# A local attention with a gated convolution on one core: one order table for all engines, transposes in 64-row pieces, two banks for products

## The chip, the cores and the metric

One core of one Trainium2 chip. The metric is device time in microseconds (us) of one execution; the profile's span runs from the first to the last instruction. Engines: PE (TensorE: matrix products, transposes), DVE (VectorE), ACT (ScalarE), POOL (GpSimd), SP (SyncE, which here issues all DMAs). Each engine has its own list of instructions, in the order in which the kernel writes them; semaphores hold an instruction until its operands are there.

## The reference

Inputs q, k, v have 4 batches, 8 heads, 768 positions, 64 channels. Each query attends to the keys less than 16 positions away and to 24 summaries, one per block of 32 positions (the maximum of the block's keys, the mean of its values). The result goes through a gated convolution.

```
k_sum = max over blocks of k;  v_sum = mean over blocks of v
scores = q k^T / 8 where |i-j| < 16;   scores_s = q k_sum^T / 8 + log(32)
a = softmax over both (sum + 1e-9);    x = a @ [v ; v_sum], heads side by side: (4, 768, 512)
gate_pre[s] = sum over t=0..4 of conv_w[t] * x[s-4+t]   (zeros ahead of position 0)
out = (sigmoid(gate_pre) * (x @ w_val)) @ w_out
```

## The kernel before

**Tiles.** A group g is a third of a batch (256 positions; 12 groups), a unit u is one half of a group's heads (4 of 8; 24 units, u = 2g or 2g+1). A query tile has 64 positions and sees 120 columns of keys: its window and the 24 summaries, laid between the keys in two halves of 12. A row of 128 partitions holds two neighbouring query tiles (e = 0 in partitions 0 to 63, e = 1 in 64 to 127); a unit has 8 such rows of scores.

**Steps of a unit**, with the letters used from here on. S: 32 products of q and k, 64 rows by 64 columns by 120, on quarters of the array, into the two banks of `s`. N: score scaling, mask and row minimum, 8 custom instructions on DVE. E: 8 exponentials with row sums on ACT. R: reciprocal on DVE. M: two multiplications by it on POOL. T: 8 transposes of 128 by 120, in two lots of four, each into the one bank of `pt`; C: a copy of each lot to SBUF on ACT. X: 32 products with v, 64 columns each. H, F: two copies of x on ACT (rounded, full); L: the rest that rounding lost, on POOL. I: the convolution's first tap on ACT, A: four more taps for each of two head pairs, 8 instructions on DVE, in the one accumulator `g`; G: tanh on ACT.

**Steps of a group.** V: x @ w_val in two halves, 24 matmuls each (three products of rounded parts); gf: gate times V on DVE; gh, gl: its rounded part on ACT, the rest on POOL; O: the product with w_out, two halves of 12 matmuls; oe: its eviction on ACT, then the store. Group 0 computes V and O in full fp32. Further: block maxima of k (`ks` on DVE, `kc` on POOL), block sums of v (a tree `tr` on POOL, transposed on PE by VS), and the conversion of the weights, which arrive as 64-bit words (ACT, DVE, POOL).

**PSUM's eight banks:** `s` two, `pt` one, `x` one, `g` one, `pp` three in turn (V, O and the sums' transposes).

**Order.** Up to unit 7 it is written out by hand (L605 to L782), from there `step(s)` (L556) runs a fixed pattern: X of unit s-2 and O or V, S of unit s, the first half of T of unit s-1, V or O, the second half of T. So PE alternates T's halves with V and O, which have the array's full shape as well. V, O and their evictions come from a queue (`proj`, L511). `early_loads` and `late_loads` set the order of the DMAs on SP.

Of the kernel before, what the change touches and what calls it, by code (L numbers as in the profile page):

```python
# [45 lines left out]
LOADS = "k0 q0 m k1 q1 n0 i k2 q2 n1 k3 q3 n2 n3 v0 c Q w0 w1 w2 w3 v1"  # L46
UPB = NTH * NHP
LOAD_K = {1: (2, 2, 4, 5)}
LOAD_VT = {1: (2, 2, 5, 6)}
PREP_K = {1: (-1,) * 4}  # L50
PREP_V = {1: (-1,) * 4}
DVE_V = ((1, 3),)
for _b in range(2, B):
    LOAD_K[_b] = tuple(_b * UPB + w for w in (-5, -4, -3, -2))
    LOAD_VT[_b] = LOAD_K[_b]
    PREP_K[_b] = tuple(_b * UPB + w for w in (-3, -2, -1, 0))
    PREP_V[_b] = tuple(_b * UPB + w for w in (-4, -3, -2, -1))


@with_exitstack  # L60
def tile_attention_then_gated_conv(
# [23 lines left out]
    ps_p = ctx.enter_context(tc.tile_pool(name="ps_p", bufs=3, space=bass.MemoryType.PSUM))  # L85
# [11 lines left out]
    ktile = {}  # L97
    vtile = {}
    vTt = {}

    def load_q0(pr):
        nc.sync.dma_start(qbd[0][:, pr], qT[0, 0, :, pr])

    def load_q(g):
        b, th = divmod(g, NTH)
        nc.sync.dma_start(qbd[g % NQB], qT[b, th])

    def load_k(b, pr):
        t = ld.tile([P, KALLOC], F32, tag=f"k{pr}", name=f"k_{b}_{pr}")
        nc.sync.dma_start(t[:, :KTOT], kT[b, pr])  # L110
        ktile[b, pr] = t

    def load_vT(b, pr):
        t = ld.tile([P, S], F32, tag="vT", name=f"vT_{b}_{pr}")
        nc.sync.dma_start(t, vT[b, pr])
        vTt[b, pr] = t

    def load_v(g):
        b, th = divmod(g, NTH)
        t = ld.tile([VROWS, TPU, DM], F32, tag="v", name=f"v_{g}")  # L120
        for e in range(VP):
            nc.sync.dma_start(t[:, 2 * e : 2 * e + 2], vw[b, th, e])
        vtile[g] = t

    def prep_k(b, pr):
        t = ktile[b, pr]
        ks = wk.tile([P, NB], F32, tag="ks", name=f"ks_{b}_{pr}")
# [6 lines left out]
        )  # L134
        for half, n in ((0, NT // 2 + 1), (1, NT // 2)):
# [5 lines left out]
    vsT = {}  # L141
    vsum = {}

    def prep_v(b, pr):
# [10 lines left out]
        vsT[b, pr] = t  # L155

    def load_vT0(i):
        t = ld.tile([P, S], F32, tag=f"k{i}", name=f"vT_0_{i}")
        nc.sync.dma_start(t, vT[0, i])
        vTt[0, i] = t  # L160

    vpad = cpool.tile([P, NPR, 2, P], F32, tag="vpad", name="vpad")
    nc.gpsimd.memset(vpad, 0.0)
    vblk = {}

    def prep_v0(i):
        half = [
            [vpad[:, i, e, off : off + HB] for off in ((OFF_A, OFF_B) if e == 0 else (OFF_B, OFF_A))]
            for e in range(2)
        ]  # L170
        src = vTt.pop((0, i)).rearrange("p (h n c) -> p h n c", h=2, c=BLK)
        for h in range(2):
            nc.vector.tensor_reduce(half[0][h], src[:, h], AX.X, ALU.add)
            nc.gpsimd.tensor_copy(half[1][h], half[0][h])

    def place_vs0():
        for e in range(2):
            ps = ps_p.tile([P, DM], F32, tag="pp", name=f"vb_{e}")
            for pr in range(NPR):
                nc.tensor.transpose(ps[:, pr * P : pr * P + P], vpad[:, pr, e], ident)  # L180
            t = cpool.tile([KW, DM], F32, tag=f"vb{e}", name=f"vb{e}")
            nc.scalar.activation(t, ps[:KW], AF.Copy, scale=1.0 / BLK)
            vblk[e] = t

    def prep_vs(b):
        ps = ps_p.tile([P, DM], F32, tag="pp", name=f"vsp_{b}")
        for pr in range(NPR):
            nc.tensor.transpose(ps[:NB, pr * P : pr * P + P], vsT.pop((b, pr)), ident)
        t = wk.tile([NB, DM], F32, tag="vs", name=f"vs_{b}", bufs=1)
        nc.scalar.activation(t, ps[:NB, :], AF.Copy, scale=1.0 / BLK)  # L190
        vsum[b] = t

    def fill_vs(g):
        b = g // NTH
        vr = vtile[g].rearrange("p (t e) c -> p e t c", e=2)
        for e in range(2):
            for half in range(2):
                off = OFF_A if (e == half) else OFF_B
                src = vsum[b][half * HB : half * HB + HB] if b else vblk[e][off : off + HB]
                nc.sync.dma_start(  # L200
                    vr[off : off + HB, e],
                    src.unsqueeze(1).broadcast_to([HB, TPU // 2, DM]),
                )
# [48 lines left out]
    def conv_cw():
        if wide:
            to_f32(cwt.rearrange("p a k -> p (a k)"), wraw.pop("cw"), NPR * NK, "cw", 1)

    acts = dict(
        k=lambda i: load_k(0, i),
        q=load_q0,
        n=load_vT0,
        w=lambda i: load_w("wv", wv, i, wk, ("gh", "gl")[i % 2]),  # L260
        o=lambda i: load_w("wo", wo, i, (cpool, cpool, wk, wk)[i], ("raw", "vpad", "xh", "xl")[i]),
        v=load_v,
        m=lambda i: nc.sync.dma_start(mask, maskc),
        i=lambda i: nc.sync.dma_start(ident, identc),
        c=lambda i: load_cw(),
        Q=lambda i: load_q(1),
    )
    for a in LOADS.split():
        acts[a[0]](int(a[1]) if len(a) > 1 else 0)

    units = [(b, th, hp) for b in range(B) for th in range(NTH) for hp in range(NHP)]
    NG = B * NTH
    st = {}
    grp = {}

    def group(g):
        if g not in grp:
            grp[g] = dict(
                xh=wk.tile([P, NPR, SG], F32R, tag="xh", name=f"xh_{g}") if g else None,
                xl=wk.tile([P, NPR, SG], F32R, tag="xl", name=f"xl_{g}") if g else None,  # L280
                gt=wk.tile([P, NPR, SG], F32, tag="gt", name=f"gt_{g}"),
                xf=wk.tile([P, NPR, HALO + SG], F32, tag="xf", name=f"xf_{g}"),
            )
            halo = grp[g]["xf"][:, :, :HALO]
            if g % NTH == 0:
                nc.gpsimd.memset(halo, 0.0)
            else:
                nc.gpsimd.tensor_scalar(
                    halo, grp[g - 1]["xf"][:, :, SG:], 1.0, 1.0, ALU.mult, ALU.mult
                )  # L290
        return grp[g]

    def mm_s(u, r):
        b, th, hp = units[u]
        g = b * NTH + th
        if r == 0:
            st[u] = dict(
# [563 lines left out]
```

## Time and profile before

| | us |
|---|---|
| runs (3): median, lowest, highest | 265.61, 263.45, 267.11 |
| profiled execution: span | 262.0 |
| PE, DVE, ACT, POOL busy in it | 231.1, 185.1, 193.0, 151.8 |

For the profiled execution the profile gives its span, from the first to the last instruction; the runs' times are of whole executions, and their median is 3.6 us above that span. A busy share is the union of an engine's instructions. The page lists a matmul with its modelled end, so what a matmul costs in a row of them is read from the chain of waits, which gives the time from one piece to the next.

### The profile page before, as it was taken

Reading aid. Unit: us, or ns where it says so; the run is one execution under the profiler, and the core shown is the slowest. Engines: PE = TensorE matmul, PEld = TensorE weight load, DVE = VectorE, ACT = ScalarE, POOL = GpSimd, SP = SyncE. Lnnn points to the kernel's source line nnn. Section 1 sums busy time; section 2 is a strip of 40 time slices with the busy share of each in tenths; the row PEclk is TensorE's granted clock in tenths of the full one; section 3 lists DMA queues with packets and bytes.
Section 4 is the critical chain, followed back from the end, with each engine's and each line's share of the span. In section 5 each row is a group of like instructions: output and inputs, shape, how many; then the busy total and the mean of one; then the engine's idle time right before and its main releaser. Section 6 shows DMA issues by size and latency. Waiting matters only on the chain.

```text
span 262.0 us, 7326 instructions
## 1 busy us (share of the span) xinstructions
PE 231.1 (88%) x2652; PEld 193.6 (74%) x2652; DVE 185.1 (71%) x692; ACT 193.0 (74%) x619; POOL 151.8 (58%) x212
## 2 busy tenths in 40 slices
PE   1258977889596999999999999999999999997994
PEld 1146866756482689888988898889889988986883
DVE  1866999597966687779776967797778667843610
ACT  1448994966648889888987898889878988875211
POOL 2243087767465788878663888887544744461410
PEclk9999999999777799999999999999999999999999
DMA  6999998175501967726118998171184511111012
GB/s 192 402 404 410 354 354 305 17 290 188 170 8 26 319 238 241 267 51 247 44 22 257 363 329 290 22 280 44 17 261 108 192 58 27 40 43 40 14 70 80
DMA packets 17028, 46.39 MB, mean 177 GB/s; under 512 B 2368, under 2 KB 3392, under 8 KB 16992
## 3 DMA queue, kind: packets, MB, share of 16 engines
q1 hardware_dynamic: 16992, 45.93, 50.9%
q8 instruction: 21, 0.34, 0.5%
q14 instruction: 15, 0.12, 0.2%
HBM read 37.46 MB, written 6.29 MB: 167 GB/s over the span
## 4 chain that ended last, share of the span: by engine, by line
PE 75%; ACT 10%; POOL 5%; issue 4%; DVE 2%; DMA 2%; SPq 0%; POOLq 0%; ACTq 0%; DVEq 0%
PE out L491 27%; PE val L453 22%; PE s L311 9%; PE x L387 8%; PE pt L367 8%; ACT p L342 4%; DMA k<-in_kT_dram 2%; POOL xl L405 2%; POOL p L354 1%; ACT pts L371 1%; DVE sn L328 1%; ACT wv L241 1%; ACT xf L403 1%; DVE ks L129 1%; POOL k L139 1%
## 5 line engine op out<-in xcount | busy, mean ns | idle before, releaser
L428 DVE SCALAR_TENSOR_TENSOR g<-xf,cwt,g 128x256 f32<-128x256 f32 x192 | 93.9, 489 | 13.9 <-ACT g L419 8.0
L342 ACT ACTIVATE p<-sn,nm 128x120 f32<-128x120 f32 x192 | 73.2, 386 | 10.9 <-DVE nm L328 10.9
L354 POOL TENSOR_TENSOR p<-p,ri 128x480 f32<-128x480 f32 x48 | 47.0, 1001 | 42.1 <-DVE ri L351 41.7
L328 DVE CUSTOM_DVE_ANT_0 sn<-s,mask 128x120 f32<-128x120 f32 x192 | 40.9, 278 | 33.3 <-PE s L311 33.3
L453 PE MATMUL val<-xh,wv 128*128 128x256 f32 x352 | 51.8, 289 | 0.7 <-ACT xh L402 0.7
L491 PE MATMUL out<-wo,gh 128*128 128x512 f32 x176 | 49.2, 418 | 2.0 <-ACT wo L241 1.2
L453 PEld LDWEIGHTS val<-xh,wv 128*128 128x128 f32 x352 | 45.6, 192 | 1.6 <-ACT xh L402 1.1
L405 POOL TENSOR_TENSOR xl<-xf,xh 128x512 fp32r<-128x512 f32 x22 | 28.3, 1288 | 23.3 <-ACT xf L403 23.3
L367 PE MATMUL pt<-ident,p 128*120 128x128 f32 x192 | 31.5, 289 | 11.0 <-ACT pts L371 7.6
L491 PEld LDWEIGHTS out<-wo,gh 128*128 128x128 f32 x176 | 32.1, 193 | 11.0 <-POOL wo L242 3.4
L311 PE MATMUL s<-k,qbd 64*64 64x120 f32 x768 | 27.7, 282 | 10.9 <-POOL k L139 10.9
L342 ACT ACTIVATION_READ_ACCUMULATOR p<-sn,nm 128x1 f32 x192 | 36.7, 191 | 0.0
L371 ACT COPY pts<-pt 120x512 f32<-120x512 f32 x48 | 27.6, 575 | 10.3 <-PE pt L367 10.3
L367 PEld LDWEIGHTS pt<-ident,p 128*120 128x120 f32 x192 | 21.7, 142 | 16.6 <-issue 7.3
L387 PEld LDWEIGHTS x<-pts,v 120*64 120x64 f32 x768 | 27.0, 141 | 9.2 <-issue 8.1
L476 POOL TENSOR_TENSOR gl<-gf,gh 128x512 fp32r<-128x512 f32 x22 | 28.5, 1298 | 6.6 <-ACT gh L467 6.6
L311 PEld LDWEIGHTS s<-k,qbd 64*64 64x64 f32 x768 | 20.9, 139 | 14.4 <-POOL k L139 12.6
L453 PE MATMUL val<-xl,wv 128*128 128x256 f32 x176 | 29.6, 288 | 1.8 <-POOL xl L405 1.7
L387 PE MATMUL x<-pts,v 120*64 120x64 f32 x768 | 30.7, 229 | 0.6 <-ACT g L419 0.5
L436 ACT ACTIVATE gt<-g 128x512 f32<-128x512 f32 x24 | 14.4, 599 | 22.0 <-DVE g L428 22.0
L153 POOL TENSOR_TENSOR vT<-vT 128x384 f32<-128x384 f32 (+3 forms) x44 | 25.6, 581 | 2.6
L453 PEld LDWEIGHTS val<-xl,wv 128*128 128x128 f32 x176 | 24.8, 191 | 2.6 <-POOL xl L405 2.1
(53 smaller groups left out, 268.2 us busy)
## 6 DMA issues: line engine op xcount, KB each, us to landing
v<-in_vw_dram SPq DMA_DIRECT2D x24, 512.0 KB
k<-in_kT_dram SPq DMA_DIRECT2D x16, 478.0 KB
vT<-in_vT_dram SPq DMA_DIRECT2D x16, 384.0 KB
out_dram<-ob SPq DMA_DIRECT2D x23, 256.0 KB
qbd<-in_qT_dram SPq DMA_DIRECT2D x11, 512.0 KB
raw_wv<-in_wv_dram SPq DMA_DIRECT2D x4, 512.0 KB
raw_wo<-in_wo_dram SPq DMA_DIRECT2D x4, 512.0 KB
v<-vs SPq DMA_DIRECT2D x36, 48.0 KB
```

The costliest lines, as they stand in the source:

```text
L311: nc.tensor.matmul(st[u]["sp"][64 * e : 64 * e + 64, h, c * KW : c * KW + KW], qbd[g % NQB][64 * h : 64 * h + 64, pr, i * QT : i * QT + QT ...
L328: nc.vector.tensor_tensor_reduce(s["sn"][:, n, :], s["sp"][:, h, c * KW : c * KW + KW], mask[:, mv, :], -1.0 / math.sqrt(D), 3.0e38, ALU.a ...
L342: nc.scalar.activation(s["p"][:, n, :], s["sn"][:, n, :], AF.Exp, bias=s["nm"][:, n : n + 1], scale=-1.0, accum_out=s["rs"][:, n : n + 1],)
L354: nc.gpsimd.tensor_tensor(s["p"][:, w], s["p"][:, w], ri[:, w].unsqueeze(2).broadcast_to([P, TPU, KW]), ALU.mult,)
L367: nc.tensor.transpose(s["pt"][:KW, i, :], s["p"][:, TPU * r + i, :], ident)
L371: nc.scalar.copy(s["pts"][:, TPU * r : TPU * r + TPU], s["pt"][:KW])
L387: nc.tensor.matmul(dst, v[:KW, i, c0 : c0 + D], src, start=True, stop=g > 0)
L405: nc.gpsimd.tensor_tensor(G["xl"][:, prs, :], x[:, prs, HALO:], G["xh"][:, prs, :].bitcast(F32), ALU.subtract)
L428: nc.vector.scalar_tensor_tensor(gt[:, r], x[:, pr, o : o + SG], cwt[:, pr, o : o + 1], gt[:, r], ALU.mult, ALU.add,)
L453: nc.tensor.matmul(pp[:, r], w, x, start=(n == 0), stop=(n == len(terms) - 1))
L476: nc.gpsimd.tensor_tensor(G["gl"][:, cos, :], gf, G["gh"][:, cos, :].bitcast(F32), ALU.subtract)
L491: nc.tensor.matmul(pp, x, w, start=(n == 0), stop=(n == len(terms) - 1))
```

## The change

All helper functions are cut into small operations, one per engine and piece, and named by a token. A table `ORDER` of 1148 tokens gives their order, for all engines and for the DMAs; a loop at the end of the kernel emits them. `step`, `proj`, the loads' functions and the order written out by hand are gone. Counts of operations stay, with these exceptions and moves:

- T: each row of a unit is transposed as two pieces of 64 rows by 120 columns, 16 per unit, all in one go. Pieces of e = 0 go to one bank, those of e = 1 to a second; `pt` has two banks in one buffer.
- C: one copy per e (half the queries of all 8 rows) instead of one per lot of four rows. X takes the tiles of e = 0 first.
- `pp` has two banks instead of three.
- N and E come in pairs, taps one by one, and the DMAs of one v tile apart, in the table's order.

```diff
-    ps_p = ctx.enter_context(tc.tile_pool(name="ps_p", bufs=3, space=bass.MemoryType.PSUM))
+    ps_p = ctx.enter_context(tc.tile_pool(name="ps_p", bufs=2, space=bass.MemoryType.PSUM))
...
-        s["pt"] = ps_t.tile([P, TPU, P], F32, tag="pt", name=f"pt_{u}_{r}")
-        for i in range(TPU):
-            nc.tensor.transpose(s["pt"][:KW, i, :], s["p"][:, TPU * r + i, :], ident)
...
-        nc.scalar.copy(s["pts"][:, TPU * r : TPU * r + TPU], s["pt"][:KW])
...
+    def op_T(u):
+        pt = once(("pt", u), lambda: ps_t.tile([P, 2, NP, QT], F32, tag="pt", name=f"pt_{u}"))
+        for n in range(NP):
+            for e in range(2):
+                w = slice(QT * e, QT * e + QT)
+                nc.tensor.transpose(pt[:KW, e, n, :], tiles["p", u][w, n, :], ident[w, w])
+
+    def op_C(u, e):
+        pts = wt(("pts", u), [KW, NP, P], "pts")
+        nc.scalar.copy(pts[:, :, QT * e : QT * e + QT], tiles["pt", u][:KW, e])
+
+    def op_X(u):
...
+        for i in (0, 2, 1, 3):
+            for r in range(2):
                 for h in range(2):
...
+    for token in ORDER.split():
+        name, *at = token.split(".")
+        ops[name](*(int(a) for a in at))
```

A token is a step's letter and its numbers: unit (or group) and piece; `k`, `q`, `n`, `v`, `w`, `o` are loads of k, q, transposed v, v, w_val, w_out, `m` the mask, `i` the identity, `f` the fill of v with block sums, `h` the convolution's halo. The table's beginning, and PE's part of it from T(9) to X(16) (a digit after the dot is the piece):

```
k.0.0 mset k.0.1 q0.0 k.0.2 q0.1 m k.0.3 q0.2 ks.0.0 n.0.1 kc.0.0 ks.0.1 q0.3 S.0.0 q.1 kc.0.1 c
ks.0.2 S.0.1 n.0.2 N.0.1 n.0.3 kc.0.2 E.0.1 N.0.0 N.0.3 w.0 N.0.2 E.0.2 i ks.0.3 S.1.0 E.0.3 n.0.0
...
PE: T.9 S.12 V.3.1 V.3.0 S.13 X.8 T.10 O.2.1 X.9 S.14 O.2.0 VS.2 T.11 S.15 X.10 V.4.1 V.4.0 T.12
X.11 S.16 T.13 O.3.1 O.3.0 S.17 T.14 X.12 V.5.1 V.5.0 S.18 X.13 O.4.1 O.4.0 S.19 T.15 X.14 V.6.0
V.6.1 X.15 T.16 S.20 O.5.0 O.5.1 VS.3 X.16
```

After X(23) PE has O.9.0 V.10.0 V.11.0 V.11.1 O.10.1 O.10.0 O.11.0 O.11.1; before, it had O, V, O, V, O, O, O there.

## Rows read from the trace of the kernel before

**Rows 1.** Page, part 1: busy time, share of the span and instructions of each engine.

```profile
PE 231.1 (88%) x2652; PEld 193.6 (74%) x2652; DVE 185.1 (71%) x692; ACT 193.0 (74%) x619; POOL 151.8 (58%) x212
```

**Rows 2.** Busy time by stretch: until X(6), until X(23), the rest; header names the columns.

```profile
core 0: us, PE busy (x) PEld busy (x) DVE busy (x) ACT busy (x) POOL busy (x), PEclk, DMA share, GB/s
0.00:89.00 89.00, 63.26 (x716) 47.01 (x718) 65.81 (x232) 60.26 (x196) 46.64 (x76) 0.92 0.68 243
89.00:235.20 146.20, 146.20 (x1804) 128.68 (x1804) 110.96 (x445) 124.69 (x410) 100.06 (x132) 1.00 0.48 161
235.20:262.00 26.80, 21.62 (x140) 17.93 (x139) 8.36 (x17) 8.04 (x15) 5.11 (x4) 1.00 0.14 50
```

**Rows 3.** Chain of waits in order of time, one steady unit: start, us, what.

```profile
106.46 1.08 PE x L387 x32
107.54 0.98 PE s L311 x32
108.52 0.58 PE pt L367 x4
109.11 2.85 PE val L453 x24
111.95 0.44 PE pt L367 x4
112.39 2.81 PE out L491 x12
115.20 1.08 PE x L387 x32
```

**Rows 4.** The same chain: X(6), X(23), the last products, the last eviction.

```profile
88.92 1.08 PE x L387 x32
...
235.81 0.69 PE x L387 x16
...
250.04 8.41 PE out L491 x36
258.52 0.39 ACT ob L500
```

**Rows 5.** Groups by line and shape, DVE: busy us, mean ns of one.

```profile
L428 DVE SCALAR_TENSOR_TENSOR g<-xf,cwt,g 128x256 f32<-128x256 f32 x192 | 93.9, 489 | 13.9 <-ACT g L419 8.0
...
L328 DVE CUSTOM_DVE_ANT_0 sn<-s,mask 128x120 f32<-128x120 f32 x192 | 40.9, 278 | 33.3 <-PE s L311 33.3
...
L129 DVE TENSOR_REDUCE ks<-k 128x24 f32<-128x768 f32 x16 | 14.9, 942 | 4.1 <-DMA k<-in_kT_dram 4.0
...
L460 DVE SCALAR_TENSOR_TENSOR gf<-gt,val 128x512 f32<-128x512 f32 x24 | 15.9, 665 | 8.9 <-ACT gt L436 3.9 <-PE val L453 3.5 <-PE out L491 1.6
```

**Rows 6.** Timeline of the start: start us, us, engine, line, operation.

```profile
3.98 0.95 DVE L129 TENSOR_REDUCE ks<-k 128x24 f32<-128x768 f32 x1 [3.98 <-DMA k<-in_kT_dram]
...
6.64 0.28 DVE L328 CUSTOM_DVE_ANT_0 sn<-s,mask 128x120 f32<-128x120 f32 x1 [1.70 <-PE s L311]
...
22.79 0.34 PE L387 MATMUL x<-pts,v 120*64 120x64 f32 x4
```

**Rows 7.** Busy time by stretch, 10 to 20 us; columns as in group 2.

```profile
10.00:20.00 10.00, 4.92 (x51) 3.46 (x43) 7.01 (x35) 4.87 (x22) 3.61 (x11) 1.00 1.03 402
```

**Rows 8.** The chain of waits: eight exponentials and their sums on ACT.

```profile
63.88 3.13 ACT p L342 x16
```

**Rows 9.** Groups by line and shape, PE weight loads of X and T.

```profile
L387 PEld LDWEIGHTS x<-pts,v 120*64 120x64 f32 x768 | 27.0, 141 | 9.2 <-issue 8.1 <-ACT g L419 0.8 <-ACT pts L371 0.4
...
L367 PEld LDWEIGHTS pt<-ident,p 128*120 128x120 f32 x192 | 21.7, 142 | 16.6 <-issue 7.3 <-POOL p L354 6.0 <-POOL vT L153 1.0
```

**Rows 10.** Timeline of PE after a wait of 3.17 us: four transposes.

```profile
69.07 1.08 PE L367 MATMUL pt<-ident,p 128*120 128x128 f32 x4 [3.17 <-ACT pts L371]
```

**Rows 11.** Busy time by stretch, 70 to 80 us.

```profile
70.00:80.00 10.00, 8.99 (x100) 7.84 (x100) 7.07 (x13) 4.31 (x9) 5.01 (x9) 0.75 0.19 70
```

More of the change, by code (lines that the diff above doesn't have):

```diff
@@ L45 @@
 FP32_G = (0,)
-LOADS = "k0 q0 m k1 q1 n0 i k2 q2 n1 k3 q3 n2 n3 v0 c Q w0 w1 w2 w3 v1"
+DVE_V = ((1, 3),)
 UPB = NTH * NHP
[L48 to L57, printed above, removed]
+ORDER = """
@@ L95, in tile_attention_then_gated_conv, with once, wt @@
     cwt = cpool.tile([P, NPR, NK], F32, tag="cwt", name="cwt")
[L97 to L101, printed above, removed]
+    wide = wv.dtype != F32
+    units = [(b, th, hp) for b in range(B) for th in range(NTH) for hp in range(NHP)]
+    NG = B * NTH
+    tiles = {}
+    def once(key, make):
+        if key not in tiles:
+            tiles[key] = make()
+        return tiles[key]
+    def wt(key, shape, tag, dt=F32, bufs=None):
+        name = "_".join(str(k) for k in key)
+        kw = {} if bufs is None else dict(bufs=bufs)
+        return once(key, lambda: wk.tile(shape, dt, tag=tag, name=name, **kw))
@@ L193, in fill_vs, with half0 @@
-    def fill_vs(g):
-        b = g // NTH
[L195 to L203, printed above, removed]
+    def half0(i, e):
+        offs = (OFF_A, OFF_B) if e == 0 else (OFF_B, OFF_A)
+        return [tiles["vpad"][:, i, e, off : off + HB] for off in offs]
@@ new lines, in op_vp @@
+    def op_vp(i, alt=0):
+        src = vTt(0, i).rearrange("p (h n c) -> p h n c", h=2, c=BLK)
+        if not alt:
+            for h in range(2):
+                nc.vector.tensor_reduce(half0(i, 0)[h], src[:, h], AX.X, ALU.add)
+            return
+        n = BLK // 2
+        while n > 1:
+            nc.gpsimd.tensor_tensor(
+                src[:, :, :, :n], src[:, :, :, :n], src[:, :, :, n : 2 * n], ALU.add
+            )
+            n //= 2
+        for h in range(2):
+            nc.gpsimd.tensor_tensor(
+                half0(i, 0)[h].unsqueeze(2), src[:, h, :, :1], src[:, h, :, 1:2], ALU.add
+            )
@@ new lines, in op_vc, with pp, op_VB, op_vb @@
+    def op_vc(i):
+        for h in range(2):
+            nc.gpsimd.tensor_copy(half0(i, 1)[h], half0(i, 0)[h])
+    def pp(key, shape):
+        name = "_".join(str(k) for k in key)
+        return once(key, lambda: ps_p.tile(shape, F32, tag="pp", name=name))
+    def op_VB(e):
+        ps = pp(("vb", e), [P, DM])
+        for pr in range(NPR):
+            nc.tensor.transpose(ps[:, pr * P : pr * P + P], tiles["vpad"][:, pr, e], ident)
+    def op_vb(e):
+        t = once(("vblk", e), lambda: cpool.tile([KW, DM], F32, tag=f"vb{e}", name=f"vb{e}"))
+        nc.scalar.activation(t, tiles["vb", e][:KW], AF.Copy, scale=1.0 / BLK)
@@ new lines, in op_VS, with op_vs, op_f @@
+    def op_VS(b):
+        ps = pp(("vsp", b), [P, DM])
+        for pr in range(NPR):
+            nc.tensor.transpose(ps[:NB, pr * P : pr * P + P], tiles["vsT", b, pr], ident)
+    def op_vs(b):
+        t = wt(("vs", b), [NB, DM], "vs", bufs=1)
+        nc.scalar.activation(t, tiles["vsp", b][:NB, :], AF.Copy, scale=1.0 / BLK)
+    def op_f(g, e, half):
+        b = g // NTH
+        vr = vtile(g).rearrange("p (t e) c -> p e t c", e=2)
+        off = OFF_A if (e == half) else OFF_B
+        src = (
+            tiles["vs", b][half * HB : half * HB + HB] if b else tiles["vblk", e][off : off + HB]
+        )
+        nc.sync.dma_start(
+            vr[off : off + HB, e], src.unsqueeze(1).broadcast_to([HB, TPU // 2, DM])
+        )
@@ L252, in conv_cw @@
[L252 to L267, printed above, removed]
@@ L339, in exps @@
-    def exps(u, r):
-        s = st[u]
-        for n in range(TPU * r, TPU * r + TPU):
+        sn = wt(("sn", u), [P, NP, KW], "sn")
+        nm = wt(("nm", u), [P, NP], "nm", bufs=4)
+        t = th * TPU + 2 * (c % 2)
+        mv = 0 if t == 0 else (2 if t == NT - 2 else 1)
+        for h in range(2):
+            n = 2 * c + h
+            nc.vector.tensor_tensor_reduce(
+                sn[:, n, :],
+                tiles["s", u][:, h, c * KW : c * KW + KW],
+                mask[:, mv, :],
+                -1.0 / math.sqrt(D),
+                3.0e38,
+                ALU.add,
+                ALU.min,
+                nm[:, n : n + 1],
+            )
@@ L433, in gate, with prs, op_H, op_F @@
-    def gate(u):
-        b, th, hp = units[u]
-        g = b * NTH + th
-        nc.scalar.activation(
-            group(g)["gt"][:, 2 * hp : 2 * hp + 2, :], st.pop(u)["gt"], AF.Tanh, scale=0.5
-        )
-    def val_mm(g, cp):
-        G = group(g)
+    def prs(u):
+        return slice(2 * (u % NHP), 2 * (u % NHP) + 2)
+    def op_H(u):
+        g = u // NHP
+        xh = wt(("xh", g), [P, NPR, SG], "xh", F32R)
+        nc.scalar.copy(xh[:, prs(u), :], tiles["x", u])
+    def op_F(u):
+        nc.scalar.copy(xf(u // NHP)[:, prs(u), HALO:], tiles["x", u])
@@ L490, in out_mm, with op_oe @@
+            terms = [(gh[:, ci, rows], w[:, ci, :]) for ci in range(4) for w in (wh, wl)]
+            terms += [(gl[:, ci, rows], wh[:, ci, :]) for ci in range(4)]
         for n, (x, w) in enumerate(terms):
-            nc.tensor.matmul(pp, x, w, start=(n == 0), stop=(n == len(terms) - 1))
-        return pp
-    def out_ev(g, si, pp):
+            nc.tensor.matmul(ps, x, w, start=(n == 0), stop=(n == len(terms) - 1))
+    def op_oe(g, si):
+        ps = tiles["out", g, si]
+        ob = wt(("ob", g, si), [P, DM], "ob")
+        hd = DM // 2
+        if (g, si) == (NG - 1, 1):
+            nc.scalar.activation(ob[:, :hd], ps[:, :hd], AF.Copy, scale=0.5)
+            nc.vector.tensor_scalar(ob[:, hd:], ps[:, hd:], 0.5, None, ALU.mult)
+        else:
+            nc.scalar.activation(ob, ps, AF.Copy, scale=0.5)
```

767 lines of the change are left out of this document (248 added, 519 removed).

## The prediction

> **What bounds the kernel now.** I read the busy shares first. PE is busy 88% of the span, DVE and ACT about 70 and 74% [rows 1]. An average hides stages, so I cut the span at the two points where the chain of waits changes character [rows 2]. Until 89 us PE is busy 63.3 us of 89, DVE 65.8, ACT 60.3: nothing is full, each waits for the others. From 89 to 235 us PE is busy 146.2 of 146.2 us, while ACT has 124.7 and DVE 111.0. The rest is the tail. The chain says the same: X(6) stands at 88.92 us, then comes one unit after another on PE alone until X(23) [rows 4]. One unit is X 1.08, S 0.98, the first half of T 0.58, V 2.85, the second half of T 0.44, O 2.81: 8.74 us [rows 3]. So there are three prices to ask for: when X(6) starts, what a unit costs on PE, and how long the tail is.
>
> **Part 1, the transposes.** Now 8 per unit, 128 columns of identity each, take 0.58 + 0.44 = 1.02 us; 0.44/4 = 0.11 each, and the four behind S cost 0.14 more than the four behind V. That 0.14 I take as the price of going from S's quarter tiles to the whole array [rows 3]. After the change there are 16 pieces with half the columns, in two halves of the array's rows, into two banks. The trace has no such piece. Bounds: X's 32 matmuls stream 64 columns, as the pieces will, two column halves side by side, at 1.08/32 = 0.034 us; S's 32, which use two row halves and two banks, take 0.98/32 = 0.031 [rows 3]. At X's price 16 pieces are 0.54 us, the entry included. From above, each piece could take a whole transpose's slot, 16 x 0.11 = 1.76 us. I take 0.54, because X's row is the nearest in columns and S's shows row halves and two banks at work together. T is now a shape of its own, so what follows it pays an entry: 0.14 more, 0.68 in all against 1.02. The gain is 0.34 per unit, some 5 us over the 15 transposes that stand after X(6).
>
> The Trainium skill, TensorEngine Tiling (Array Packing), Tiling Modes, Key Properties, says that a change of tiling mode drains the engine, which speaks against this change. The trace agrees: 0.58 against 0.44 [rows 3].
>
> **Part 2, the order until X(6).** Counts of operations stay as they are but for the pieces. DVE is the engine that the table loads most here. T(8) and S(11) stand before X(6) on PE, so DVE must have come to the last score reduce of unit 10. Until 89 us the old kernel had run 64 score reduces, 48 taps, 8 block maxima and 5 gates on DVE; the table asks up to that point for 86, 40, 10 and 4. That is 22 x 0.213 - 8 x 0.489 + 2 x 0.942 - 0.67 = +2.0 us [rows 5], a score reduce at 40.9/192 = 0.213, so 67.8 us of work. DVE starts at 3.98 us [rows 6], hence 71.8 without idle time, against 23.2 us of idle time before.
>
> Following the table with these durations I find waits of 6.5 us. The mask now comes behind three loads of k instead of one: the list up to it holds 1.91 MB, and at 402 GB/s [rows 7] the first score reduce can start at about 8.1 us against 6.64 [rows 6]. v of group 0 lands at about 23, behind q(2), w(2) and k(1,1), and X(0) starts at about 23.5, against 22.79 [rows 6]; S, four units ahead by then, hides that. The other waits are for ACT, which sets up one tap accumulator at a time. So unit 10's reduce ends at 78.3, S(11) at 79.4. T(8) is next, and now waits for both copies of unit 7, since there is one transpose buffer (of two banks). ACT's list up to that copy is its 60.3 us less the table load and a few conversions, plus 14 more exponentials at 3.13/8 = 0.39 [rows 8], about 62.6. It starts at 8.5 and waits some 9.5 us in my walk, three of them for O(0,0), which can't start before DVE has joined the last word of w_out at 58 us. The copy ends at 80.6, and X(6) starts at about **81.3 us, 7.6 earlier**. PE idles there from 54 to 58. After such a wait of 3.17 us four transposes took 1.08 us instead of 0.58 [rows 10], at a granted clock of 0.75 over that stretch, a mean of its two levels, 1.2 and 2.4 GHz [rows 11]. The same may happen again; DVE, not PE, sets the pace there, so I cost it at nothing, with 2 us for the upper end if that cover is gone.
>
> **Part 3, X(6) to X(23).** The table holds, on PE between them, 17 X, 12 S, 15 T, 15 V, 17 O and 2 sets of sum transposes: 18.4 + 11.8 + 15 x 0.68 + 42.8 + 47.8 + 0.9 = 131.9 us, against 146.2. Of the 14.3, 5 is Part 1, and 9 is work that now stands before X(6) or after X(23). The added waits: products have two banks, not three, so a V or O waits for the eviction of the one before last, and behind it in PE's queue stand the next S and T; T(u) waits for both copies of u-1, and behind it stand X and V. Walking X(6) to X(16), the banks come free in time (at O(2,0) by 0.7 us), but T(10), T(11) and T(12) wait 0.4 to 0.9 us each for ACT's second copy, because ACT waits for the eighth tap before each tanh. X(12) to X(16) is clear. For the whole stretch I take 7 us of waits, 3 found and 4 for handoffs between engines that the walk took as instant. ACT fits: its list here is some 131 us, so it could be through at 80.6 + 131 = 212. X(23) starts at 81.3 + 138.9 = **220.2**, against 235.2.
>
> DMA: 150 issues on SP, as before, in another order; that queue is busy 48% in this stretch [rows 2], and no load of the walk is late. POOL has 144 operations as before, and 100 of 146 us [rows 2]; nothing.
>
> **Part 4, the tail.** After X(23) there are now 3 V and 5 O (one O more): 1.08 + 8.55 + 14.05 = 23.7 us. V(10,0) waits about 0.9 for the gate of V(10,1), which stands on DVE behind six taps of unit 22. Now the last product ends at 250.04 + 8.41 = 258.45 [rows 4], and 3.55 us follow until the span's end at 262.0. Together 28.2.
>
> **The sum.** 220.2 + 28.2 = 248.4 us of span. The profiled execution has 262.0 and the median of the runs is 265.6, 3.6 above; added, **252 us**.
>
> **The rivals.**
> *A piece costs a whole slot.* If weight loads of the two halves go one behind the other and nothing overlaps, T costs 1.76 + 0.14 + 0.14 = 2.04, 1.36 more than I took, and with 15 on the path, 252 + 20 = **272 us**, slower than before. It decides from 0.09 us per piece on (15 x 0.91 eats the 13.6 us). For it: a weight load of T takes 142 ns, one of X, with half the columns, 141, so the records don't say how much room there is [rows 9]. Against it: loads of that length stand in X and S too, at 0.034 and 0.031 per matmul. Chance 0.09.
> By the Trainium skill, TensorE: Matmul & The Clock Gate, LDWEIGHTS (loading the stationary operand), a load's time goes with its columns, at P/1.2 ns, whatever the rows: 120 columns give 100 ns, 16 loads 1.6 us per unit. That is an estimate from the page, and by it this rival's time would be about 270. No row here separates loads of 64 and 128 rows with the same columns.
>
> *The pieces gain nothing.* At half of 0.11 each, one after another, T costs 0.88 + 0.28 = 1.16, 0.48 more than I took: +7, **259 us**. Chance 0.18.
>
> *The start stays as it is.* If waits of one engine for another eat the order's gain (an in-order queue with small pieces has more places to wait), X(6) stays at 88.9, +7.6, and the waits of Part 3 double, +4 to +7: **264 to 266 us**, no change. For it: the old start left 23 us of DVE unused too. Against it: my walk follows the table itself. Chance 0.20.
>
> *The waits vanish.* With no waits in Part 3 and half of those in Part 2: 252 - 7 - 3 = **242 us**. For it: ACT has 131 us of work there, so nothing forbids it. Chance 0.13.
>
> **How the numbers follow.** My forecast has 0.40: 252 us, its own range 247 to 257. The range for 8 in 10 goes down to 243, leaving half of the last rival out, and up to 264, taking in the second rival, the 2 us of clock and half of the third, with the first left out. A measurement of this kernel tells about 2%, 5.3 us, from no change: faster is under 260.3, slower over 270.9. Forecast, last rival and most of the second are faster: 0.40 + 0.13 + 0.15 = 0.68. No change: the third, the rest of the second, and a first rival of half size: 0.24. Slower: 0.08.
>
> **What would show it.** The chain of the changed kernel has X(6) near 81 us; DVE is busy over 0.85 of the stretch before. PE's unit is near 8.4 us, and the line of T shows 16 pieces in about 0.5 us; 0.9 or 1.8 there means the second or the first rival. In the waits, T behind ACT's copy, and V or O behind DVE's gate, sum to no more than 7 us after X(6). I am wrong if PE has gaps of more than a microsecond in each unit, or if the time before X(6) is not shorter.

## The result, and the profile after

| | before | after |
|---|---|---|
| median of the runs, us | 265.66 | 247.46 (246.18 to 250.54) |
| profiled execution: span | 262.0 | 245.8 (its own time 247.61) |
| X(6) starts | 88.9 | 82.65 |
| X(6) to X(23) | 146.2 | 135.8 |
| X(23) to the end of the span | 26.9 | 27.35 |

The ratio is 0.9305 [0.9234, 0.9375]: 18 us less, faster. The forecast was 252 us, with a range of 243 to 264. In the spans, 6.2 us of the gain lie before X(6) and 10.4 between X(6) and X(23); the tail takes 0.4 more. That is 16.2; the other 2 us are there because the profiled execution of the kernel before, with 262.0 of span and the some 1.8 around it that the other runs have, was faster than the median of its runs. In some executions a kernel takes a few per cent longer at a lower granted clock; two of e9's runs (278.66, 278.85) and two of e8's (252.67, 252.87) are such, so the medians of these two stand too high.

Busy shares after, answering to [rows 1]:

```profile
PE 221.6 (90%) x2844; PEld 187.2 (76%) x2844; DVE 181.7 (74%) x692; ACT 190.6 (78%) x619; POOL 152.6 (62%) x212
```

Busy time by stretch after, cut at X(6) and X(23), and two short stretches, which answer to [rows 2, 7, 11]; columns as there:

```profile
0.00:82.60 82.60, 63.31 (x940) 49.99 (x940) 68.83 (x280) 64.34 (x224) 50.12 (x83) 1.00 0.81 287
82.60:218.40 135.80, 134.38 (x1744) 116.49 (x1740) 102.30 (x392) 118.20 (x381) 94.71 (x124) 1.00 0.48 156
218.40:245.80 27.40, 23.86 (x165) 20.69 (x164) 10.55 (x21) 8.02 (x15) 7.76 (x6) 0.99 0.16 57
...
10.00:20.00 10.00, 5.29 (x87) 3.89 (x80) 8.71 (x54) 7.75 (x38) 3.13 (x10) 1.00 1.04 401
70.00:80.00 10.00, 9.97 (x121) 9.43 (x118) 9.67 (x49) 9.38 (x36) 6.20 (x10) 1.00 0.55 176
```

In the first stretch PE is busy as long as before, DVE 3.0 and ACT 4.1 us longer, in 6 us less. PE stays full after X(6). In the last row PE is full and has 1.00 of its clock where it had 0.75.

The chain of waits after, one steady stretch and the tail (start, us, what), answering to [rows 3, 4]:

```profile
120.07 1.08 PE x L467 x32
121.16 0.98 PE s L397 x32
122.14 0.61 PE pt L450 x16
122.75 5.78 PE out L550 x24
128.53 0.98 PE s L397 x32
129.51 0.62 PE pt L450 x16
130.13 1.08 PE x L467 x32
131.21 5.85 PE val L521 x48
...
218.52 1.08 PE x L467 x32
219.60 2.99 PE out L550 x12
222.59 8.48 PE val L521 x72
231.07 11.21 PE out L550 x48
242.30 0.39 ACT ob L557
```

Sixteen pieces of T take 0.61 us where eight whole transposes took 0.58 + 0.44. Most O and most V now have both halves together.

The start after, on DVE and PE (timeline), answering to [rows 6]:

```profile
3.95 0.95 DVE L244 TENSOR_REDUCE ks<-k 128x24 f32<-128x768 f32 x1 [3.95 <-DMA k<-in_kT_dram]
...
10.28 0.28 DVE L413 CUSTOM_DVE_ANT_0 sn<-s,mask 128x120 f32<-128x120 f32 x1 [0.56 <-PE s L397]
...
7.53 1.08 PE L397 MATMUL s<-k,qbd 64*64 64x120 f32 x16 [7.53 <-DMA qbd<-in_qT_dram]
9.14 1.08 PE L397 MATMUL s<-k,qbd 64*64 64x120 f32 x16 [0.53 <-DMA qbd<-in_qT_dram]
...
27.88 0.49 PE L467 MATMUL x<-pts,v 120*64 120x64 f32 x4
...
59.68 1.12 PE L550 MATMUL out<-wf,gf 128*128 128x512 f32 x2 [0.52 <-DVE wf L362]
...
62.65 1.13 PE L550 MATMUL out<-wf,gf 128*128 128x512 f32 x2 [0.27 <-DVE wf L362]
...
82.65 0.57 PE L467 MATMUL x<-pts,v 120*64 120x64 f32 x12
```

The first score reduce starts 3.6 us later than before and X(0) 5.1 us later, and still X(6) comes 6 us earlier.

### The profile page after: what moved, and what is told of

Same layout as the page of the kernel before. It is cut to its first block, busy times and chain, and to the rows that moved or that the text cites. A ratio compares the mean times of both kernels' runs of the same rounds, so it can differ in the third digit from the quotient of the medians.

```text
span 245.8 us, 7708 instructions
## 1 busy us (share of the span) xinstructions
PE 221.6 (90%) x2844; PEld 187.2 (76%) x2844; DVE 181.7 (74%) x692; ACT 190.6 (78%) x619; POOL 152.6 (62%) x212
## 4 chain that ended last, share of the span: by engine, by line
PE 56%; DVE 26%; ACT 10%; issue 4%; DMA 3%; SPq 1%; POOL 0%; DVEq 0%; ACTq 0%
PE val L521 19%; PE out L550 17%; DVE g L501 10%; PE s L397 8%; PE x L467 6%; DVE sn L413 6%; ACT p L428 4%; PE pt L450 3%; DMA qbd<-in_qT_dram 3%; DVE wf L362 2%; DVE wf L353 2%; DVE ks L244 2%; ACT g L496 2%; DVE gf L526 2%; ACT pts L454 1%
## 5 line engine op out<-in xcount | busy, mean ns | idle before, releaser
L501 DVE SCALAR_TENSOR_TENSOR g<-xf,cwt,g 128x256 f32<-128x256 f32 x192 | 93.2, 485 | 31.1 <-ACT g L496 16.2
L428 ACT ACTIVATE p<-sn,nm 128x120 f32<-128x120 f32 x192 | 73.6, 389 | 11.6 <-DVE nm L413 10.2
L441 POOL TENSOR_TENSOR p<-p,ri 128x480 f32<-128x480 f32 x48 | 48.5, 1019 | 30.9 <-DVE ri L436 27.3
L413 DVE CUSTOM_DVE_ANT_0 sn<-s,mask 128x120 f32<-128x120 f32 x192 | 43.3, 275 | 10.0 <-PE s L397 6.8
L521 PE MATMUL val<-xh,wv 128*128 128x256 f32 x352 | 49.9, 283 | 0.0
L550 PE MATMUL out<-wo,gh 128*128 128x512 f32 x176 | 45.6, 401 | 0.0
L521 PEld LDWEIGHTS val<-xh,wv 128*128 128x128 f32 x352 | 44.5, 188 | 1.3 <-DVE g L501 0.3
L397 PE MATMUL s<-k,qbd 64*64 64x120 f32 x768 | 30.4, 299 | 16.3 <-DMA qbd<-in_qT_dram 8.1
L487 POOL TENSOR_TENSOR xl<-xf,xh 128x512 fp32r<-128x512 f32 x22 | 28.3, 1290 | 20.0 <-ACT xf L482 10.2
L397 PEld LDWEIGHTS s<-k,qbd 64*64 64x64 f32 x768 | 23.1, 150 | 21.7 <-POOL k L257 8.2
L535 POOL TENSOR_TENSOR gl<-gf,gh 128x512 fp32r<-128x512 f32 x22 | 28.2, 1292 | 9.0 <-ACT gh L530 9.0
L521 PE MATMUL val<-xl,wv 128*128 128x256 f32 x176 | 27.8, 279 | 0.0
L550 PE MATMUL out<-wo,gl 128*128 128x512 f32 x88 | 24.1, 395 | 0.0
L496 ACT ACTIVATE g<-x,cwt 128x256 f32<-128x256 f32 x40 | 18.0, 449 | 7.5 <-DVE g L501 3.3
L507 ACT ACTIVATE gt<-g 128x512 f32<-128x512 f32 x24 | 14.4, 600 | 11.2 <-DVE g L501 11.0
```

Source lines behind the costliest of these rows:

```text
L397: nc.tensor.matmul(sp[64 * e : 64 * e + 64, h, c * KW : c * KW + KW], qbd[g % NQB][64 * h : 64 * h + 64, pr, i * QT : i * QT + QT], ktile( ...
L413: nc.vector.tensor_tensor_reduce(sn[:, n, :], tiles["s", u][:, h, c * KW : c * KW + KW], mask[:, mv, :], -1.0 / math.sqrt(D), 3.0e38, ALU.add,
L428: nc.scalar.activation(p[:, n, :], tiles["sn", u][:, n, :], AF.Exp, bias=tiles["nm", u][:, n : n + 1], scale=-1.0, accum_out=rs[:, n : n + 1],
L441: nc.gpsimd.tensor_tensor(p[:, w], p[:, w], ri[:, w].unsqueeze(2).broadcast_to([P, TPU, KW]), ALU.mult)
L487: nc.gpsimd.tensor_tensor(xl[:, prs(u), :], xf(g)[:, prs(u), HALO:], tiles["xh", g][:, prs(u), :].bitcast(F32), ALU.subtract,)
L501: nc.vector.scalar_tensor_tensor(gt, xf(u // NHP)[:, pr, o : o + SG], cwt[:, pr, o : o + 1], gt, ALU.mult, ALU.add)
```

## The experiments

Each line: the median, the ratio to the kernel before as it ran beside it, with its interval, and X(6), X(6) to X(23) of its profiled execution. In two kernels whose part before X(6) is that of the changed kernel, X(6) stood at 80.64 and 81.94 against 82.65; less than 2 us at that point says nothing.

| run | median | ratio | X(6) | X(6)–X(23) |
|---|---|---|---|---|
| the change | 247.46 | 0.9305 [0.9234, 0.9375] | 82.65 | 135.8 |
| e1, whole transposes | 250.57 | 0.9449 [0.9378, 0.952] | 81.51 | 140.0 |
| e2, one half, then the other | 250.46 | 0.9449 [0.9375, 0.9523] | 82.14 | 141.3 |
| e7, plain order in X | 247.82 | 0.9326 [0.9261, 0.9392] | 81.61 | 136.5 |
| e9, old order, pieces | 277.09 | 1.0492 [1.0406, 1.0578] | 88.35 | 156.1 |
| e11, old order, two banks | 274.73 | 1.0381 [1.033, 1.0433] | 91.61 | 154.8 |
| e3, q and mask first | 247.12 | 0.9316 [0.9263, 0.937] | 81.42 | 136.1 |
| e4, no low words | 244.19 | 0.92 [0.9138, 0.9262] | 79.37 | 136.4 |
| e6, both | 242.15 | 0.9122 [0.9071, 0.9174] | 76.50 | 136.5 |
| e8, sums on POOL | 250.87 | 0.9365 [0.9278, 0.9452] | – | – |
| e5, old order, PE kept busy | 263.13 | 0.9953 [0.991, 0.9996] | 87.33 | 146.1 |
| e10, shorter V | 246.85 | 0.9319 [0.9262, 0.9376] | 80.64 | 135.4 |
| e12, and fewer taps | 244.46 | 0.9203 [0.9125, 0.9281] | 81.94 | 133.5 |

### What the pieces are worth (e1, e2, e7, e9, e11)

**e1** keeps the changed kernel's order and banks, with whole transposes of 128 rows:

```diff
-            for e in range(2):
-                w = slice(QT * e, QT * e + QT)
-                nc.tensor.transpose(pt[:KW, e, n, :], tiles["p", u][w, n, :], ident[w, w])
+            dst = pt[:KW, n // TPU].rearrange("p (n two) c -> p n (two c)", two=2)[:, n % TPU]
+            nc.tensor.transpose(dst, tiles["p", u][:, n, :], ident)
```

> The changed kernel's order and banks, but each row of a unit is transposed whole again (8 of 128 rows, four per bank, one copy per bank, X in the old order of tiles). It tells the pieces' share from the order's. Theory of the forecast: PE sets the time from X(6) on and pieces save 0.34 us of each of the 15 transposes there, so 5 to 7 us slower than the changed kernel, 252 to 254 us. Second theory, from the time between first matmuls in the two traces (T and its share of the next entry 0.15 to 0.2 cheaper): 2 to 4 us slower, 249 to 251. Rival, PE does not set the time: under 1.5 us, 247 to 249.

**e2** keeps the pieces and puts the loop over e outside: eight of one row half, then eight of the other.

```diff
-        for n in range(NP):
-            for e in range(2):
+        for e in range(2):
+            for n in range(NP):
```

> The changed kernel, but the eight pieces of the lower half are issued before the eight of the upper, so that no two row halves work side by side. Theory: the two halves of the array stream at the same time, a pair of pieces takes 0.058 us, and issued apart each piece takes that, so T goes from 0.61 to about 1.05 us and the time up by 5 to 9 us, to 252 to 256. Rival: a piece costs 0.03 us because that is the pace of issue, whatever half it is on: T stays at 0.6 and the time within 1 us of 247.5.

The chain of e1, then that of e2, at the place of the rows above:

```profile
122.00 1.02 PE pt L449 x8
123.01 5.60 PE out L550 x24
```

```profile
124.34 0.90 PE pt L450 x16
125.24 5.78 PE out L550 x24
```

Whole transposes cost 1.02 instead of 0.61, but the O behind them costs 5.60 instead of 5.78: they have its shape, so it pays no entry. Net, that is 0.23 at this place; over the whole stretch from X(6) to X(23) it is 4.2 us, 0.28 for each of the 15 T, 12 of which have S or X behind them, and 3.1 us of the median. So the order with its new banks carries 15 of the 18 us, by difference.

e2 has the same pieces, the same copies and the same banks, and loses as much. What makes pieces cheap is that the two row halves alternate: in the changed kernel's records most pairs of pieces start 3 to 4 ns apart, and a pair follows every 58 to 60 ns. In e2 a piece that runs alone starts 58 to 59 ns behind the last one; in most lots three pairs in the middle still start within 8 ns of each other, so a lot takes 0.90 and not the 1.05 expected. Each row half writes a bank of its own, so the banks alternate with the halves; which of the two counts, no run separates.

**e7** takes X's tiles in plain order again (`for r`, then `for i`).

> The changed kernel with X in the plain order of tiles, so that its second product already needs ACT's second copy. Theory: on PE each X stands at least one other piece behind its copies except in a few units, so nothing is lost: within 1 us of 247.5. Rival: X waits for the second copy in each unit, 0.3 us or more over 18 units: 5 us slower.

Nothing: 247.82. The order of X within a unit is no part of the gain.

**e9** puts the pieces into the old order, lot by lot, with two banks for `pt` and two for `pp`; since two banks can't hold three products, V(1,1) is moved behind O(0,1). **e11** is its control: the same without the pieces.

```diff
-    ps_p = ctx.enter_context(tc.tile_pool(name="ps_p", bufs=3, space=bass.MemoryType.PSUM))
+    ps_p = ctx.enter_context(tc.tile_pool(name="ps_p", bufs=2, space=bass.MemoryType.PSUM))
...
-    ppv.append(val_mm(1, 1))
...
+    ppv.append(val_mm(1, 1))
```

> The kernel before with the pieces alone: each lot of four rows is transposed as eight pieces of 64 rows into two banks, one copy per lot; products have two banks, and V(1,1) is moved behind O(0,1), which two banks need. Theory: each of the two lots stands between V and O, so a unit now pays four more entries of about 0.1 to 0.14 us for a streaming time cut from 0.88 to 0.47; the pieces gain nothing in the old order, and the time is within 1.5 us of the same kernel with whole transposes (the run beside it). Rival: the pieces are worth here what they are in the new order, 3 us less than the run beside it.

> The kernel before with two banks for products instead of three, and V(1,1) behind O(0,1); transposes whole, in one bank. It is what the run with the pieces in the old order is held against, and it prices the third bank. Theory: V and O alternate with 0.6 us of transposes between, and their evictions take 0.6 us, so two banks do from unit 8 on; 0 to 2 us slower than before for the V that is moved, 265.5 to 267.5. Rival: evictions come late and PE waits in each unit, 0.3 us or more: over 270.

One unit in the chain of e9:

```profile
107.28 0.98 PE s L311 x32
108.26 0.38 PE pt L369 x8
108.63 3.02 PE val L458 x24
111.66 0.38 PE pt L369 x8
112.04 3.00 PE out L496 x12
```

The pieces take 0.76 us per unit instead of 1.02 [rows 3], but V costs 3.02 instead of 2.85 and O 3.00 instead of 2.81: 0.17 + 0.19 for going back to the full array. The sum is 0.10 more per unit, 1.7 us for 17 units; measured, 156.1 against 154.8. The whole times show no difference: e9's two lower runs took 273.27 and 275.52, e11's four 274.30 to 275.20. In the old order pieces gain nothing, since each lot stands between products. The changed kernel has one lot per unit, and 12 of its 15 T after X(6) have S or X behind them.

e11 refutes what I expected of the third bank. Taking it away, with the moved V(1,1), costs 3.8% in the old order, 10.8 us between the medians of the runs side by side (274.73 and 263.92). Of this, 8.6 us lie between X(6) and X(23). That stretch of e11, the time behind PE's first wait in it, and PE's waits in it (us in total, times, longest):

```profile
91.60:246.40 154.80, 149.82 (x1801) 131.25 (x1800) 110.75 (x445) 125.21 (x409) 100.09 (x132) 0.98 0.47 151
...
135.90:140.50 4.60, 4.60 (x14) 3.40 (x16) 0.76 (x1) 1.04 (x2) 1.79 (x4) 0.63 0.21 31
```

```profile
PE out L491 <- DVE gf L460: 5.0, 2, 2.5
```

PE idles 5 us in it, where it had no gap [rows 2], at two places, before 135.85 and before 193.15 us. Each time the granted clock was lower over some 5 us behind (0.63, 0.67), and the O there took 4.62 and 4.25 us instead of 2.81. These two units, from X to X, took 13.47 and 13.11 us, where the kernel before had 9.16: 8.2 of the 8.6 us, 5.0 of waiting and 3.2 in the two O. Both are units in which VS takes a bank of `pp` between V and O. With two banks O then needs the bank of the V just ahead, and that V's gate stands behind eight taps on DVE. No other unit has such a wait. So the rival's time came out, but not its mechanism, a wait in each unit.

The new order runs with two such banks, and PE is busy 134.38 of 135.80 us in it. In its table both VS of this stretch stand behind an O, whose bank ACT frees, and V(3) stands ahead of O(2), V(4) ahead of O(3), so that a gate has units of other work to come in. That this is why two banks are enough there is read from the table; no run shows it.

### What bounds the start (e3, e4, e6, e8)

**e3** loads the first q and the mask ahead of the other tiles of k, and puts the first score reduces ahead of the block maxima.

```diff
-k.0.0 mset k.0.1 q0.0 k.0.2 q0.1 m k.0.3 q0.2 ks.0.0 n.0.1 kc.0.0 ks.0.1 q0.3 S.0.0 ...
+k.0.0 mset q0.0 m k.0.1 q0.1 k.0.2 q0.2 k.0.3 n.0.1 q0.3 q.1 c n.0.2 n.0.3 w.0
+i n.0.0 ks.0.0 kc.0.0 S.0.0 N.0.1 E.0.1 N.0.0 ks.0.1 kc.0.1 S.0.1 ...
```

> The changed kernel with the first loads in the old order (first k, first q, mask, then the rest) and unit 0's first scores ahead of the later block maxima on DVE. The first score reduce moves from 10.3 to about 6.7 us. Theory: DVE sets the pace from there to X(6), so X(6) and the end come 1.5 to 3 us earlier, 244.5 to 246. Rival: later waits (loads of v, ACT) take it back: within 1 us of 247.5.

**e4** leaves out the low three bits of each word of w_val and w_out: 8 instructions of DVE fewer, the joins replaced by plain shifts.

```diff
+        if nm != "cw":
+            return
...
+        if nm != "cw":
+            nc.vector.tensor_scalar(d, sc.bitcast(U32), 3, None, ALU.logical_shift_left)
+            return
```

> The changed kernel with the low words of the two weight matrices left out (the lowest three mantissa bits of w_val and w_out are zero): eight DVE instructions of 0.78 and 0.94 us fall away before X(6), 6.8 us. Theory: DVE sets the pace until X(6), so X(6) comes 4 to 7 us earlier and, as PE sets the time from there on, the end 3 to 6 us earlier, 241.5 to 244.5. Rival: ACT or the chain through the tap accumulator sets the pace, DVE idles instead: within 1.5 us of 247.5.

**e6** does both.

> The changed kernel with the low words of both weight matrices left out and the first loads in the old order, both together. Alone, the first gave 3.3 us and the second 0.3. Theory: DVE's work until X(6) is what bounds the start, so with that work gone the earlier first scores still bring little: 243 to 244.5 us. Rival: each hid the other, and together they give 5 us or more: under 242.5.

By the medians e3 alone gives 0.3 us, e4 3.3, both together 5.3; by the ratios nothing, 2.8 and 4.9. The first stretch of e6, and the last 20 us ahead of X(6) in the changed kernel:

```profile
0.00:76.50 76.50, 60.49 (x940) 48.59 (x941) 61.73 (x272) 64.06 (x225) 47.61 (x83) 1.00 0.87 309
```

```profile
62.60:82.60 20.00, 19.92 (x262) 15.84 (x262) 18.73 (x79) 18.87 (x66) 14.78 (x22) 1.00 0.72 233
```

In e6 X(6) has moved by 6.15 us and DVE's work by 7.1. In the changed kernel PE waits at 62.65 for DVE's last join of w_out, as the timeline above shows, and from there to X(6) PE is busy 19.92 of 20.0 us and ACT 18.87. In e3, e10 and e12 this wait ends at 61.44, 60.64 and 61.96, and X(6) comes 20.0 us later each time. So DVE's conversions set when the last 20 us begin, and PE's and ACT's lists fill them. The earlier first score reduce of e3 does not move the last join beyond what two profiles differ by.

That e6 lies 2 us under e4 does not show that the early start is worth something once the conversions are shorter. The profiled execution of e4 had a granted clock of 0.5 from 50.7 to 54.1 us, behind a wait of PE of 1.81 us, and the one run of e4 with a mean clock of 1.0 took 242.75, 0.6 above e6's median. e6 is the fastest of all, but leaves the low bits out.

**e8** is e3 with two of DVE's sums (`vp.1`, `tr.1.3`) moved to POOL.

> The changed kernel with the first loads in the old order and two block sums of v (pair 1 of batch 0, pair 3 of batch 1) moved from DVE to POOL as trees of additions: 1.9 us less on DVE before X(6), nothing left out. Theory: DVE bounds the start, half of its work given up came back as time in the run without low words (3.3 of 6.8), so 0.5 to 1.5 us faster than the changed kernel, 246 to 247. Rival: the trees delay POOL's multiplications and cost as much: 247.5 or more.

Median 250.87, ratio 0.9365 [0.9278, 0.9452], lowest run 248.18: no gain is shown. Its one profile is of the run at 252.67, so where the time went stays open.

### How much is the clock (e5)

**e5** is the kernel before with 28 and 14 transposes of the identity into a bank of `pp`, where PE was idle at some 66 and 80 us.

```diff
+    def fill(n, nm):
+        ps = ps_p.tile([P, DM], F32, tag="pp", name=f"fill_{nm}")
+        for _ in range(n):
+            nc.tensor.transpose(ps[:, :P], ident, ident)
```

> The kernel before, with 28 and 14 transposes of the identity that nobody reads, put where PE stood idle at 66 to 69 us and 80 to 82 us. Its trace had the granted clock at 0.5 (1.2 GHz) from 68.1 to 75.0 and from 81.8 to 88.6 us; the changed kernel's has none. Theory: the half clock was on the path, so with PE kept busy both windows go, X(6) comes 2 to 4 us earlier and the time is 262 to 264 us, and that much of the change's gain was clock, not order. Rival: ACT and POOL set the pace there, X(6) stays within 1 us of 88.9 and the time within 1 us of 265.7.

One stretch of the kernel before, and the same of e5:

```profile
70.00:75.00 5.00, 4.90 (x45) 4.41 (x45) 3.04 (x5) 2.73 (x6) 2.77 (x4) 0.50 0.38 139
```

```profile
70.00:75.00 5.00, 4.07 (x45) 3.45 (x42) 3.33 (x5) 3.21 (x7) 3.78 (x5) 1.00 0.37 134
```

The clock stays at 2.4 GHz where it had gone to 1.2 GHz. X(6) comes 1.5 us earlier, no more than two profiles differ by, and the ratio is 0.9953 [0.991, 0.9996], just under 1. So of the change's 18 us some 1.2, and at most 2.4, are clock: its order leaves PE no gap over 1.4 us after the first 20 us, where the kernel before had one of 3.17 [rows 10].

### What bounds the rest (e10, e12)

**e10** leaves out the last four of V's twelve terms in groups 6 to 9, 7.6 us of PE work.

```diff
-                terms += [(wh[:, ci, cs], xl[:, ci, :]) for ci in range(4)]
+                if g not in (6, 7, 8, 9):
+                    terms += [(wh[:, ci, cs], xl[:, ci, :]) for ci in range(4)]
```

> The changed kernel with the last 4 of 12 terms of V left out in groups 6 to 9 (the product with what rounding x lost): 8 halves of V, each 8 matmuls of 0.118 us shorter, 7.6 us of PE between X(12) and X(23), nothing on ACT or DVE. Theory: PE sets the time from X(6) on, so the end comes 6 to 7.6 us earlier, 240 to 241.5. Rival: ACT, with 117 us of work in the 135 us from X(6) to X(23), is as near, and the taps' chain through one accumulator with it: 4 us or less, 243.5 to 246.

X(12) to X(23), where the edit lies, went from 88.4 to 87.5 us; the median fell by 0.6, the ratio not at all (0.9319). Waits of the changed kernel from 82 to 218 us (engine, line, waited for: us in total, times, longest):

```profile
DVE g L501 <- ACT g L496: 12.0, 15, 3.5
...
ACT gt L507 <- DVE g L501: 7.3, 8, 2.7
```

And of e10:

```profile
DVE g L501 <- ACT g L496: 11.5, 14, 3.5
...
ACT gt L507 <- DVE g L501: 7.8, 9, 2.7
...
PE out L551 <- DVE gf L527: 2.8, 3, 1.2
```

The work taken from PE came back as waits of PE, 7.2 us in all against 1.3, of which 2.8 were for the gate. ACT waits for the eighth tap, DVE for the next first tap, and both hand over through the one accumulator `g`.

**e12** shortens that chain too: in units 12 to 19, two of the four taps of each head pair are left out.

```diff
+        if 12 <= u <= 19 and o >= 2:
+            return
```

> As e10 (a third of the terms of V left out in groups 6 to 9, 7.6 us of PE work), and besides, in units 12 to 19, the last two of the four taps of each head pair left out: 32 taps of DVE, 32 x 0.489 = 15.6 us of its work. Theory (after X(6) two chains are equally long, PE's list and the chain first tap, taps, tanh between ACT and DVE, which goes through the one accumulator g; in e10 only the first was shortened, and that gave 0.6 us): with both shortened the time falls by 4 to 7 us against e10's 246.85, to 240 to 242.5, and X(12) to X(23) falls from 87.5 to some 82; ACT's waits for the taps (7.8 us) fall below 4. Rival (it is ACT's own list of operations, which the edit leaves as it is, or the sum of handoffs): 245.5 or more, and ACT busy over 0.9 of that stretch.

244.46, between the two. Its waits from 81 to 214 us:

```profile
DVE g L503 <- ACT g L496: 17.0, 14, 5.6
...
ACT gt L509 <- DVE g L503: 3.6, 5, 2.7
...
PE out L553 <- DVE gf L529: 1.9, 2, 1.0
```

ACT's wait for the taps fell from 7.8 to 3.6, as the theory had it. But X(12) to X(23) became 85.1 us, not 82, and DVE now waits longer for ACT. ACT is busy 72.6 of these 85.1 us, 0.85, below the rival's 0.9, and PE still idles 4.2. So PE and the tap chain are about equally long, and a third limit lies 3 us below them. Fewer taps alone were not run, so the tap chain's own share is not shown apart. That it is ACT's list, which stands in order between the copies of T and the first taps, is argued from these waits, not shown.

## Why the prediction was right, and where it was not

**Part 1 held.** T was forecast at 0.54 plus 0.14 for what follows. It measured 0.61 to 0.62 and 0.17 to 0.19 (e9), where a V or an O follows. The gain was to be 0.34 per unit; e1 puts it at 0.28 on the mean of 15 T. By the Trainium skill, TensorE: Matmul & The Clock Gate, LDWEIGHTS (loading the stationary operand), 16 loads, one behind the other, would take an estimated 1.6 us. The trace does not agree: loads and transposes together took 0.61, and in e2 even pieces that ran alone came every 58 to 59 ns, not 100.

Both rivals on the pieces are out by the chain's rows. But "the pieces gain nothing", put at 1.16 us per unit with entries, is what e9 shows: 0.76 + 0.17 + 0.19 = 1.12. Which of the two cases holds depended on what stands behind a lot, and the prediction charged 0.14 whatever stands there. Its 0.88 for pieces one after another, too, is what e2 came to (0.90).

**Part 2 came out 1.4 us late**, at 82.65 for 81.3, less than two profiles differ by. T(8) did wait for the second copy of unit 7: it started 0.10 us after it, and so in e3, e4, e6, e10 and e12. DVE's work up to there is 68.83 us (67.8 forecast), and DVE was busy 0.83 of the stretch, not over 0.85. The step that failed is "DVE, not PE, sets the pace there". The last word of w_out was joined at 62.6 us, not 58, and from there on PE was as full as ACT. With the 20.0 us behind it, a join at 58 would have let PE's list end at 78; with the join at 62.6 it ended together with ACT's. That the time still came out near was in part luck.

DVE's first score reduce started at 10.28, not 8.1. The mask was not what it waited for: it takes the second half of S(0), whose q tile, issued behind three tiles of k, let PE start only at 9.14. X(0) came at 27.88, not 23.5. That PE might fall to half its clock, with 2 us set aside, did not happen: the waits for the joined weights broke up into gaps of 0.3 to 0.5 us, and the granted clock stayed at 1.00. (The 1.08 us of [rows 10] is a timeline's span; its like at full clock, at 22.21 us of the same trace, is 0.65, not the chain's 0.58.) Groups by line and shape, two conversions on DVE, after and then before:

```profile
L353 DVE TENSOR_SCALAR wf<-raw_wv 128x512 uint32<-128x512 uint32 x4 | 3.1, 776 | 0.0
...
L362 DVE SCALAR_TENSOR_TENSOR wf<-sc_wv,wf 128x512 uint32<-128x512 uint32 x4 | 3.1, 775 | 0.0
```

```profile
L216 DVE SCALAR_TENSOR_TENSOR wf<-sc_wv,wf 128x512 uint32<-128x512 uint32 x4 | 2.8, 692 | 0.4
...
L215 DVE TENSOR_SCALAR wf<-raw_wv 128x512 uint32<-128x512 uint32 x4 | 1.7, 420 | 0.0
```

The same instructions take longer in the fuller stretch, nearly 3 us over the 16 of both weights (14.1 against 11.2 us), against the 4.6 us by which the last join was late; the forecast took them at their old durations. In the records of both kernels, those with no operation of POOL beside them took 0.42 us (shift) and 0.69 (join), and all that took over 0.73 had one beside them for more than 0.9 of their time. So had some of the short ones, and no run takes POOL's work away, so this is not shown to be the cause.

**Part 3: near in sum, by errors that cancelled, and with one claim wrong.** Work of 131.9 and waits of 7 made 138.9; the trace has 135.8. PE idles only 1.4 of it (135.80 less 134.38), so the waits were put 5.6 us too high and the work 2.5 too low: from one piece's start to the next, less idle time, V and O took 93.5 us instead of 90.6, T 9.3 instead of 10.2. T(10), T(11) and T(12) did wait, 0.1 to 0.2 each instead of 0.4 to 0.9. The failed step is that PE alone sets the time and "ACT fits". Adding to PE costs (e1, e2), but taking 7.6 us off it gives 0.9 in this stretch (e10). PE was full because the table spaces its work to the pace of the tap chain as well; that is argued from e10 and e12. The prediction compared ACT's summed work (131 us; busy in the trace 118.2) with PE's, and no sum shows that two engines wait for each other in turn.

**Part 4** says "3 V and 5 O (one O more)". The 3 and 5 are right; what is added is one V, since the kernel before had 2 V and 5 O there. The wait of 0.9 for the gate did not come: 27.35 instead of 28.2.

**The rest of the sum.** 1.8 us lie around the span (247.61 against 245.8), not 3.6; the other 1.8 were that the profiled execution of the kernel before was faster than the median of its runs. With 2.6 us of span that makes the 4.5 between 252 and 247.46. The rival "the start stays" is out (X(6) is 6.2 us earlier), and "the waits vanish" was nearly true of PE's waits after X(6) (1.4 of the 7), but the work there was longer, and X(6) came later than forecast, not earlier.

## What to carry to other kernels

Price a change of a tile's shape with what stands behind it: the same pieces gave 0.28 us for each T where 12 of 15 have S or X behind them, and lost 0.10 per unit where each lot stands between full-array products. A full engine is not proof that it sets the time: take work off it as well as putting work on, since two lists that hand over to each other can be as long. A buffer's worth belongs to an order: a third bank was worth 8.6 us after X(6) to the old one, nearly all of it in two units, and the new one did without it.

## What was unexpected of the hardware

- Two row halves of the array, fed in turn, transposed a pair every 58 to 60 ns; one half after the other, a piece that ran alone took 58 to 59 ns. So a pair costs what one piece costs.
- Going back to the full array costs V 0.17 and O 0.19 us behind T (e9), near the 0.14 between S and T that [rows 3] showed.
- Two waits of PE of 2.5 us each cost the old order with two banks 8.2 us, since the granted clock was 0.63 and 0.67 in the 5 us behind them and the two O there took 3.2 us longer (e11).
- 28 and 14 transposes of an identity, put into gaps of PE, kept the granted clock at 1.00 where it had been 0.50 (e5).
- Integer shifts on DVE took 0.776 us on the mean instead of 0.420, with the same shape, in the stretch where the other engines were busier; the long ones all ran beside operations of POOL.
